# A planner change in a spectral filter + GEGLU kernel: filter-row gathers planned after the transfer transposes, and no charge for waiting on one's own engine

## The chip, the cores and the metric

The kernel runs on one core of a Trainium2 chip. The metric is the device time of one execution in microseconds (us), median of the fast executions.

## The reference, cut to what matters

```python
def reference(A_x, A_w_r, A_w_i, B_x, B_w_gate, B_w_up, B_w_down):
    x  = A_x                                   # (1, 2048, 512) bf16
    xn = _layernorm(x, axis=-1)                # no scale, no shift
    W  = w_r + 1j * w_i                        # (2048, 257) filter
    a  = irfft2(rfft2(xn) * W)                 # over both axes
    g, u = xn @ w_gate, xn @ w_up              # 512 -> 1792
    b  = (gelu(g, approximate=True) * u) @ w_down
    return x + a + b
```

## The kernel before: the parts that matter

The 2048 rows are 16 "columns" of 128 rows. VectorE makes the statistics of a column (`st`), aggregates them (`mv`), adds epsilon to the variance (`ve`); GpSimd takes the power -1/2 (`rstd`); VectorE normalises (`xn`). The columns 0 to 3 are transposed by TensorE, the others by DMA transfers. Then there are two branches: gate, up and down products, and the two-dimensional Fourier filter, built of matmuls (`bp`, `dp`, `ep`, then backwards `gp`, `yp`).

The kernel's operations are not written in the order in which they run. A planner in the source, a list scheduler with a model duration for every operation, simulates the engines and emits the operations in the order that its simulation gives:

```python
class _Plan:
    HOP = 0.1
    ...                                                     # cut
    def run(self):
        ...                                                 # cut
                for o in ops:
                    if any(d.end is None for d in o.deps):
                        continue
                    at = max([d.end + d.lag + self.HOP for d in o.deps if d.eng != "PE" or o.eng != "PE"] + [0.0])
                    ...                                     # cut: buffers, lanes; then the best priority wins
    ...
    order = plan.run()
    with tc.manual_schedule():
        for o in order:
            o.fn()
```

`at` is the planner's time at which an operation may start. It fixes only the place of the operation in its engine's queue. On the chip each engine works through its queue in order and waits for the data that an instruction really needs.

The three kinds of operation that the argument needs, with their model durations, are the normalisation chain, the fold and the gathers. The fold is four VectorE operations of 128x1024 that prepare four columns for the transform (`A`, `A`, `xf`, `xf`), followed by four groups of four `bp` matmuls that read `xf`:

```python
    def layernorm(c0, n, due, after=(), halves=1):
        for c in range(c0, c0 + n):
            s = dve(0.6, lambda c=c: stats(c), [XD[c]] + list(after), due - 3.0 + 0.01 * (c - c0))
            ag.append(dve(0.15, ..., (s,), due - 3.2))      # aggregate
        e = dve(0.07, ..., ag, due - 5)                     # ve
        r = add("POOL", 0.55, ..., (e, o_mem[1]), due - 5, lag=0.1)   # rstd: the power
        ...                                                 # then one normalisation per column, deps (r,)

    def fold(cg, t):
        ...
        a0 = dve(0.61, f0, deps, t, new=(ab,))
        a1 = dve(0.61, f1, deps + [a0], t, use=(ab,))
        a2 = dve(0.61, f2, (a0, a1), t, new=(xb,), use=(ab,))
        a3 = dve(0.61, f3, (a2,), t, use=(ab, xb))
        for q in range(4):
            ...
            p = pe(0.222, mm, (a2, a3, d_rf), t + 1, new=(sb,), use=(xb,))     # bp
            PS_[cg, q] = act(0.53, ev, (p,), t - 5, use=(sb,))                 # Bs

    for k in range(2):
        for c, s, a, n in ((2, 1, 0, 7 * KC), (0, 0, 0, KC), (1, 1, 7 * KC, KC)):
            d_tw.append(dma(P * n * 2, lambda k=k, c=c, s=s, a=a, n=n: gather(k, s, c, a, n),
                            [g_idx] + XN[11], 20, eng="POOL", issue=1.2))
```

## Time and profile before

| | before |
|---|---|
| device time | 179.18 us, three runs from 179.08 to 179.73 |
| span of the profile | 177.6 us |
| TensorE busy | 173.4 us, 1100 matmuls |
| VectorE, ScalarE, GpSimd busy | 118.1, 87.4, 18.6 us |
| idle time of TensorE | 1.34 before its first matmul, 2.68 in the tail, 0.17 in between |

### The profile page before, as it was taken

What the parts mean: (1) busy time and instruction counts of PE and PEld (TensorE: products, weight loads), DVE (VectorE), ACT (ScalarE), POOL (GpSimd) and SP (SyncE); (2) the same over time, 40 slices, a digit from 0 to 9 for tenths busy, and PEclk for the clock granted to TensorE, in tenths of its full rate; (3) what the DMA queues carried; (4) which work ended last, traced back from release to release, by engine and by line L of the source; (5) the groups of instructions that cost most, each with busy time, mean ns of one, the idle gap of its engine ahead of it and who ended that gap; (6) DMA issues with size and microseconds to landing.
All of it is one profiled execution on the core that took longest, in us unless ns stands there. A gap on an engine that the chain in (4) does not pass through costs nothing.

```text
span 177.6 us, 3041 instructions
## 1 busy us (share of the span) xinstructions
PE 173.4 (98%) x1100; PEld 92.9 (52%) x1100; DVE 118.1 (66%) x266; ACT 87.4 (49%) x158; POOL 18.6 (10%) x33
## 2 busy tenths in 40 slices
PE   6999999999999999999999999999999999999993
PEld 2598545545554544554555455554445444544463
DVE  1869999999537995889999885336442541632522
ACT  3162437456789737999998855453111211211100
POOL 3212138743200000000000000000000000000000
PEclk9999999999999999999999999999999999999999
DMA  5999487999297001302211121100222221322212
GB/s 144 311 355 359 86 270 84 223 296 193 52 347 255 2 0 29 93 2 59 61 48 37 37 59 37 27 0 0 84 68 66 83 89 59 92 80 69 74 45 59
DMA packets 23182, 19.24 MB, mean 108 GB/s; under 512 B 8512, under 2 KB 21824, under 8 KB 23168
## 3 DMA queue, kind: packets, MB, share of 16 engines
q1 hardware_dynamic: 22176, 17.57, 35.0%
q0 software_dynamic: 320, 1.19, 3.1%
q10 hardware_dynamic: 672, 0.30, 0.6%
q8 instruction: 8, 0.13, 0.3%
q14 instruction: 6, 0.05, 0.1%
HBM read 13.28 MB, written 2.10 MB: 87 GB/s over the span
## 4 chain that ended last, share of the span: by engine, by line
PE 91%; ACT 3%; DVE 3%; issue 1%; POOL 0%; DVEq 0%; POOLq 0%
PE u_ps L502 25%; PE g_ps L502 25%; PE warm L380 3%; ACT E L652 2%; PE yp L818 2%; PE bp L581 2%; PE gp L767 2%; PE yp__2078 L872 2%; PE yp__1994 L872 2%; PE yp__1967 L872 2%; PE yp__1936 L872 2%; PE yp__1909 L872 2%; PE yp__1820 L872 2%; PE yp__1793 L872 2%; PE yp__1762 L872 2%; PE yp__1735 L872 2%
## 5 line engine op out<-in xcount | busy, mean ns | idle before, releaser
L502 PE MATMUL g_ps<-xnT,Wg_sb 128*128 128x512 bf16 (+2 forms) x264 | 58.1, 347 | 0.0
L502 PE MATMUL u_ps<-xnT,Wu_sb 128*128 128x512 bf16 (+2 forms) x264 | 57.9, 347 | 0.0
L527 DVE TENSOR_TENSOR hT<-u_ps,ge 128x512 bf16<-128x512 f32 x56 | 38.4, 685 | 17.5 <-PE u_ps L502 14.4
L519 ACT ACTIVATE ge<-g_ps 128x512 bf16<-128x512 f32 x56 | 33.5, 598 | 30.5 <-PE g_ps L502 26.5
L502 PEld LDWEIGHTS <-Wu_sb 128*128 128x128 bf16 x264 | 24.3, 98 | 22.3 <-DMA Wu_sb<-in_B_w_up_dram 0.2
L502 PEld LDWEIGHTS <-Wg_sb 128*128 128x128 bf16 x264 | 24.3, 98 | 20.7 <-issue 0.2
L872 PEld LDWEIGHTS <-hT 128*128 128x128 bf16 x252 | 23.0, 98 | 21.9
L824 ACT CAST yf<-yp 128x512 bf16<-128x512 f32 x16 | 9.3, 586 | 37.6 <-PE yp L818 37.6
L652 ACT CAST E<-ep 64x512 bf16<-64x512 f32 x32 | 18.5, 579 | 1.1 <-PE ep L646 0.7
L396 DVE BATCH_NORM_STATS2 st<-x_t 128x6 f32<-128x512 bf16 x16 | 10.5, 676 | 4.8 <-DMA x_t<-in_A_x_dram 4.8
L629 ACT CAST ds<-dp 128x512 bf16<-128x512 f32 x16 | 8.8, 589 | 1.1 <-PE dp L624 1.0
L773 ACT CAST Gs<-gp 128x512 bf16<-128x512 f32 x16 | 8.6, 593 | 1.0 <-PE gp L767 1.0
L406 POOL TENSOR_TENSOR rstd<-ve,half 128x2 f32<-128x2 f32 (+2 forms) x7 | 6.6, 949 | 21.9 <-DVE ve L404 21.9
L585 ACT CAST Bs<-bp 128x512 bf16<-128x512 f32 x16 | 8.3, 603 | 0.5 <-PE bp L581 0.5
L818 PEld LDWEIGHTS <-Gs 128*128 128x128 bf16 x64 | 4.8, 98 | 3.5
L380 PE MATMUL warm<-warm 128*128 128x512 bf16 (+1 forms) x14 | 5.1, 539 | 1.3 <-POOL half L373 1.3
L412 DVE TENSOR_SCALAR xn<-x_t,mv,rstd 128x512 bf16<-128x512 bf16 (+1 forms) x17 | 6.1, 399 | 0.3 <-POOL rstd L406 0.3
L818 PE MATMUL yp<-CT,Gs 128*128 128x128 bf16 x64 | 6.0, 219 | 0.0
L683 DVE TENSOR_TENSOR m<-X,TW 128x1024 bf16<-128x1024 bf16 x8 | 5.5, 692 | 0.2
L624 PEld LDWEIGHTS <-Bs 128*128 128x128 bf16 x64 | 4.4, 98 | 2.4
L689 DVE TENSOR_TENSOR m<-X,TW 128x1024 bf16<-128x1024 bf16 x8 | 5.5, 684 | 0.0
L646 PE MATMUL ep<-ds,CT 128*128 128x512 bf16 x16 | 5.4, 379 | 0.0
(103 smaller groups left out, 169.0 us busy)
## 6 DMA issues: line engine op xcount, KB each, us to landing
y<-in_A_x_dram SPq DMA_DIRECT2D x16, 128.0 KB, 2.1
F<-F SPq DMA_DIRECT2D x32, 64.0 KB, 2.0
out_dram<-y SPq DMA_DIRECT2D x15, 128.0 KB, 1.7
Wd_sb<-in_B_w_down_dram SPq DMA_DIRECT2D x2, 896.0 KB, 8.3
x_t<-in_A_x_dram SPq DMA_DIRECT2D x3, 512.0 KB, 6.8
Wg_sb<-in_B_w_gate_dram SPq DMA_DIRECT2D x2, 512.0 KB, 6.8
Wu_sb<-in_B_w_up_dram SPq DMA_DIRECT2D x2, 512.0 KB, 9.1
Wg_sb<-in_B_w_gate_dram SPq DMA_DIRECT2D x3, 256.0 KB, 5.1
```

What stands on the lines that cost most here:

```text
L380: nc.tensor.matmul(tiles["warm"][:, 0:w], lhsT=warm[:, 0:P], rhs=warm[:, 0:w], start=True, stop=True)
L396: V.bn_stats(out=st[:], in_=x_t[:, c])
L502: nc.tensor.matmul(tiles[f"{nm}.{key}"][:, f * w:f * w + w], lhsT=W[:, e, (f0 + f) * P:(f0 + f + 1) * P], rhs=rhs(e), start=(f + e == 0), ...
L519: nc.scalar.activation(out=e[:, 0:nf * w], in_=tiles[f"g_ps.{key}"][:, 0:nf * w], func=AF.Gelu_apprx_tanh)
L527: V.tensor_tensor(out=out, in0=tiles[f"u_ps.{key}"][:, 0:nf * w].rearrange("p (f w) -> p f w", w=w) if nf > 1 else tiles[f"u_ps.{key}"][:, ...
L585: nc.scalar.copy(out=o, in_=tiles[f"bp.{cg}.{q}"][:].rearrange("p c (r g a) -> p (c r) g a", r=2, a=4))
L629: nc.scalar.copy(out=ds[:].rearrange("p (s k t) -> p s k t", s=2, t=2), in_=tiles[f"dp.{G}"][:].rearrange("p s t k -> p s k t"))
L652: nc.scalar.copy(out=tiles[f"E.{g}"][64 * h:64 * h + 64, r], in_=tiles[f"ep.{g}.{h}"][64 * r:64 * r + 64])
L773: nc.scalar.copy(out=o, in_=tiles[f"gp.{g}.{h}"][:].rearrange("p q (n a) -> p (q n) a", a=4))
L818: nc.tensor.matmul(yp[:, q], lhsT=tiles["G"][:, q, c], rhs=IQ[q], start=(q == 0), stop=(q == 3), skip_group_check=True)
L824: nc.scalar.copy(out=tiles[f"yf.{c // 2}"][:, c % 2], in_=tiles[f"yp.{c}"][:])
L872: nc.tensor.matmul(y[:, s], lhsT=tiles[sb, f][:, cl * P:(cl + 1) * P], rhs=Wd_sb[:, f, s], start=(f == 0), stop=False)
```

## The change

The intent was to keep GpSimd and the transfer rings free for the transposes that the gate and up products wait for (gathers after the last transposes, part A), and to correct a planner that charged a hand-over of 0.18 us (lag 0.08, hop 0.1) even where producer and consumer are neighbours in one engine's queue (part B). No load changes.

```diff
@@ in _Plan.run
-                    at = max([d.end + d.lag + self.HOP for d in o.deps if d.eng != "PE" or o.eng != "PE"] + [0.0])
+                    at = max([d.end + (0.0 if d.eng == o.eng and not d.nbytes else d.lag + self.HOP)
+                              for d in o.deps if d.eng != "PE" or o.eng != "PE"] + [0.0])
@@ gathers
             d_tw.append(dma(P * n * 2, lambda k=k, c=c, s=s, a=a, n=n: gather(k, s, c, a, n),
-                            [g_idx] + XN[11], 20, eng="POOL", issue=1.2))
+                            [g_idx] + [o for t in range(12, NC) for o in XT[t]], 20, eng="POOL", issue=1.2))
```

## The prediction

> **What bounds the kernel now.** I read the page's busy shares first, then busy time by stretch, then the chain of work that ended last, and only then the time-ordered instructions of GpSimd and VectorE, where the change acts.
>
> ```profile
> PE 173.4 (98%) x1100; PEld 92.9 (52%) x1100; DVE 118.1 (66%) x266; ACT 87.4 (49%) x158; POOL 18.6 (10%) x33
> ```
>
> TensorE is busy 173.4 of 177.6 us; nothing else is above 66%. The stretches (length, then busy time per engine) say where the missing 4.2 us lie:
>
> ```profile
> 0.00:1.34 1.34, 0.00 (x0) 0.00 (x1) 0.00 (x0) 0.00 (x0) 0.80 (x8) 1.00 0.00 0
> 5.78:11.50 5.72, 5.67 (x85) 5.10 (x85) 3.79 (x12) 2.06 (x4) 1.27 (x2) 1.00 1.08 327
> ...
> 27.10:36.00 8.90, 8.90 (x67) 5.00 (x65) 8.79 (x20) 5.51 (x11) 6.82 (x7) 1.00 0.85 163
> 36.00:45.00 9.00, 9.00 (x56) 4.58 (x54) 8.96 (x19) 5.46 (x11) 4.23 (x13) 1.00 1.03 228
> ...
> 69.00:85.00 16.00, 15.88 (x98) 8.17 (x97) 12.68 (x31) 15.67 (x29) 0.00 (x0) 1.00 0.23 54
> ...
> 172.00:177.60 5.60, 2.92 (x42) 2.63 (x39) 1.34 (x4) 0.00 (x0) 0.00 (x0) 1.00 0.16 47
> ```
>
> TensorE stands idle 1.34 us before its first matmul, 0.05 us in the start, 0.12 us at 69 to 85, and 2.68 us in the tail, where the last tile is added and stored. That is 4.19, all of it. VectorE is full from 27 to 45 (8.79 of 8.90, 8.96 of 9.00) without costing TensorE anything; ScalarE is full at 69 to 85 and costs 0.12. Four gate or up matmuls of 128x512 take 0.86 us in the chain, 0.216 each, at a granted clock of 1.00: this is the matmul rate and not padding. The chain leaves TensorE in one place in mid-kernel (start, length, piece):
>
> ```profile
> 63.31 0.74 PE u_ps L502 x4
> 64.05 0.34 DVE Y L693
> ...
> 75.36 0.59 ACT ds L629
> 75.99 0.38 PE gp L767 x4
> ```
>
> So the order of VectorE and ScalarE work around the first filter groups is what sits closest to the limit.
>
> **What the Trainium skill says.** (1) "Perfetto Trace Analysis", section "Identifying the Most-Contended Engine", warns that matmul busy share is a poor measure of nearness to the roofline. Here the constant 0.216 us per 512 columns shows the work is real, so I keep the reading. (2) "DMA: Bandwidth & Descriptors", section "Anatomy of one DMA", fits a transfer issued from GpSimd as 2.0 us plus bytes / 436e3. For a large gather (128 x 1799 x 2 bytes = 460 KB) that estimates 3.1 us; the trace has 3.7 to 6.2 us from issue to landing, median 4.7, and I use the trace. (3) "VectorE: DVE Perf Modes", section "The DRAIN you can't avoid", has semaphores between VectorE operations add nothing. The trace differs slightly: two independent 128x1024 additions start 0.60 us apart (42.16, 42.76), the next, which needs their result, 0.72 us later (43.48). (4) "SBUF — State Buffer", section "Who interferes with whom", has GpSimd and VectorE locking each other out of a shared port. A power over 128x4 took 1.98 us at 25.19 and 1.04 at 37.99, which fits, though VectorE was no slower during the gathers.
>
> **The change, part by part.** The kernel is a list of operations that a small planner in the source orders before emission. The planner's dependences place an operation in its engine's queue; the chip waits only for the data. So nothing is added to or removed from the chip's work: the same 1100 matmuls, the same transfers, in another order. There are two edits.
>
> *Part A, the gathers.* Six gathers of filter rows are planned after the last four transfer transposes instead of after the normalised columns 8 to 11. GpSimd now (start, length):
>
> ```profile
> 27.36 1.23 POOL L364 DMA_INDIRECT TW<-in_A_w_r_dram,idx_t  x1 [0.19 <-issue]
> ...
> 34.68 0.95 POOL L364 DMA_INDIRECT TW<-in_A_w_i_dram,idx_t  x1 [0.30 <-issue]
> 37.99 1.04 POOL L406 TENSOR_TENSOR rstd<-ve,half 128x4 f32<-128x4 f32 x1 [2.36 <-DVE ve L404]
> ...
> 43.32 0.92 POOL L611 TENSOR_TENSOR tt<-TW 128x8 f32<-128x8 bf16 x2 [1.44 <-DMA TW<-in_A_w_i_dram]
> 44.21 1.28 POOL L613 TENSOR_SCALAR TW<-tt 128x8 bf16<-128x8 f32 x4
> ```
>
> Today they take 34.68 + 0.95 - 27.36 = 8.27 us, then the last power and the table fix follow. With the new order the power comes first. A gather touches no transposed data, so on the chip it needs no landing of a transpose: it starts when the power ends, at 37.99 + 1.04 = 39.0. Issue ends at 47.3; the last starts at 46.35 and lands at 51.0 to 52.6 (4.7 to 6.2). The last two subtractions and four scalings take 45.49 - 43.32 = 2.2 us, so the fixed table is ready at 53.2 to 54.8 instead of 45.5. Its first reader:
>
> ```profile
> 55.63 0.69 DVE L683 TENSOR_TENSOR m<-X,TW 128x1024 bf16<-128x1024 bf16 x1
> ```
>
> Slack 0.8 to 2.4 us. The planner is also more pessimistic than the chip: it charges 1.2 us per gather after the transposes have landed and queues their bytes behind the down weights, so I estimate it places this multiplication at 58 to 63 of its own time. The table is therefore there first, and the price is that group 0's filter may end up to some 3 us later. Is that covered? The last inverse product (gp) of the last group runs at 114.54, the first final product (yp) that needs it at 116.72, and gate/up work lasts to 119.5; then the down projection of a column has 14 matmuls (3.02 us) that need no filter result, and the four gate/up PSUM buffers let four columns start, 12 us. A slip of 3 us is well inside. Cost on the path: 0.
>
> *Part B, no hop on the same engine.* In the planner an operation no longer waits lag plus hop (0.08 + 0.1 = 0.18 us) for one on its own engine. On the chip this wait did not exist, so nothing is saved as such; chains are just put back to back where another operation used to be slipped in. Each true dependence that becomes adjacent costs up to 0.12 us of VectorE. With 16 statistics, 16 aggregates and four folds in the full stretch, perhaps 20 new ones give at most 2.4 us, 2% of VectorE's 118. Against it: the seven row-0 operations of group 0 close up, so its filter, begun later, ends not much later than today's 68.8. The gate/up multiplications keep the highest priority and, with two PSUM buffers each, may be late: the one at 37.85 ends at 38.54, while the second-next write of such a buffer starts near 40.2, so 1.6 us late is free.
>
> At the very start order does matter:
>
> ```profile
> 5.24 0.18 DVE L403 BATCH_NORM_AGGREGATE mv<-st 128x2 f32<-128x6 f32 x1
> 5.38 0.60 DVE L412 TENSOR_SCALAR xn<-x_t,mv,rstd 128x256 bf16<-128x256 bf16 x2
> 5.90 0.15 DVE L404 TENSOR_SCALAR ve<-mv 128x1 f32<-128x1 f32 x1
> ```
>
> Working through the planner's rule by hand, the tiny variance addition (5.90) becomes ready directly after the aggregate and goes ahead of the normalisation. An addition after its aggregate starts 0.22 us later (4.23 to 4.45) and the next operation 0.07 after that, so the normalisation starts at 5.24 + 0.29 = 5.53 instead of 5.38: 0.15 us later, and TensorE waited for it (the first transposes began at 5.78, as the warm-up ended). The second column's chain is earlier by some 0.4 us, which can fill part of it. On the path: 0 to +0.15 us.
>
> Sum: 179.18 + 0 (gathers) + 0.05 to 0.15 (start) + 0 to 0.2 (new small gaps at 69 to 85) - at most 0.17 (the two gaps of today) = 179.0 to 179.5; I take 179.3.
>
> **Rivals.** *The table becomes the wait.* If the down weights' 1.8 MB, issued at 47.7, delay the last gather by 3 us or more, the table comes at 57 or 58; a VectorE queue held at that multiplication holds the gate/up multiplications, TensorE runs dry 1.6 us later, and 1 to 4 us are lost: 180 to 183. For it: DMA share 0.72 at 45 to 55. Against: the planner puts the reader later too. About 4%. *ScalarE becomes the bound.* It is 98% busy at 69 to 85; if filter groups 0 and 1 release their buffers together, copies and Gelus bunch, with gaps of 0.3 to 1 us: 179.5 to 180.2. About 15%. *The gathers were in the way and leave it.* They overlap the transposes of columns 8 to 11 and a full VectorE; moved out, VectorE could get ahead. TensorE does not wait there, so it brings at most 0.2 us: 179.0. About 30%.
>
> **Range and chances.** A gain of 2% is 3.6 us, of which reorder-able idle time offers 0.17; only the fixed start or tail could give more, and no edit touches them: 0.01. A loss of 2% takes the first rival at nearly full size: 0.03. The rest is 0.96. The three runs before spread over 0.65 us, hence a range from 178.8 to 180.4, longer upwards since all waiting can only be added.
>
> **What would show it.** Right: TensorE busy stays at 173.4 within 0.5; gathers start at about 39 directly behind the last power; the table fix ends at 53 to 55; the first table multiplication waits for VectorE's own work and not for GpSimd; the last gp lies at 114 to 118; the variance addition precedes the first normalisation. Wrong: a wait of VectorE on the table fix with TensorE idle beside it, TensorE gaps above 0.5 us at 55 to 90, gathers starting only after 43 (a wait that I think absent), or a shift of the first gate matmul (6.89) by more than 0.3 us.

## The result, and the profile after

| | before | after |
|---|---|---|
| device time, median of 6 runs | 179.39 (179.08 to 180.01) | 180.18 (179.95 to 180.51) |
| ratio after / before | | 1.0041, 95% interval 1.002 to 1.0063 |
| span of the profile | 177.6 | 178.7 |

Ratios in this document are the mean time of one kernel's fast runs over that of the other's of the same rounds, so not quite the ratio of the medians quoted. Executions over 1.5% slower than the fastest of the same kernel are left out of the means. The change is within 2%, but it is a small loss: 0.0041 x 179.4 = 0.74 us. The predicted sum, 179.0 to 179.5, has no room for it. When the two were run again in another job (e6 below) the ratio was 1.0019, with an interval from 0.9983 to 1.0054, so by times alone the loss is clear of noise in this first job only.

The busy shares of the changed kernel come first:

```profile
PE 171.9 (96%) x1082; PEld 92.4 (52%) x1100; DVE 119.4 (67%) x266; ACT 87.4 (49%) x158; POOL 16.8 (9%) x33
```

The trace has 1082 of the 1100 matmul records but all 1100 weight loads. So 171.9 is too low by 18 missing records and must not be read as less work or more idleness. Idle time has to be found as gaps between starts instead. The stretches of the changed kernel (bounds, length, then busy time of TensorE, weight loads, VectorE, ScalarE, GpSimd, clock, DMA share, GB/s) answer to those that the prediction quotes of the kernel before:

```profile
5.78:11.50 5.72, 5.05 (x80) 4.50 (x80) 4.39 (x14) 1.99 (x4) 1.29 (x2) 1.00 1.11 326
...
27.10:36.00 8.90, 8.85 (x66) 5.01 (x66) 8.83 (x19) 6.55 (x13) 0.00 (x0) 1.00 0.77 133
36.00:45.00 9.00, 8.52 (x51) 4.14 (x51) 8.60 (x18) 4.44 (x9) 6.49 (x6) 1.00 0.90 202
...
69.00:85.00 16.00, 15.78 (x87) 7.82 (x88) 15.59 (x39) 12.38 (x23) 0.00 (x0) 1.00 0.19 45
```

GpSimd is empty from 27.1 to 36 and works from 36 to 45: the gathers have moved. TensorE was busy 9.00 of 9.00 from 36 to 45 before and is 8.52 now, and VectorE, still full, has 0.40 idle. The place is visible in TensorE's time-ordered list (start, length of the group, engine, line, operation, in square brackets a wait and what ended it). Before:

```profile
41.03 1.03 PE L502 MATMUL g_ps<-xnT,Wg_sb 128*128 128x512 bf16 x4
41.89 1.06 PE L581 MATMUL bp<-RF_t,xf 128*128 128x128 bf16 x16
42.78 1.03 PE L502 MATMUL u_ps<-xnT,Wu_sb 128*128 128x512 bf16 x4
```

After:

```profile
41.38 1.03 PE L503 MATMUL g_ps<-xnT,Wg_sb 128*128 128x512 bf16 x4
42.63 0.40 PE L582 MATMUL bp<-RF_t,xf 128*128 128x128 bf16 x4 [0.22 <-DVE xf L564]
43.23 0.84 PE L582 MATMUL bp<-RF_t,xf 128*128 128x128 bf16 x12 [0.21 <-DVE xf L568]
43.91 1.03 PE L503 MATMUL u_ps<-xnT,Wu_sb 128*128 128x512 bf16 x4
```

A group's length includes the pipeline's end, so the next group starts earlier than start plus length: four gate matmuls take 0.86 us from start to next start (41.03 to 41.89), sixteen `bp` 0.89, hence four some 0.22. After the change the `bp` place in the queue comes at 41.38 + 0.86 = 42.24 and its first four start at 42.63: 0.39 us idle. The other twelve could follow at 42.63 + 0.22 = 42.85 and start at 43.23: 0.38 us. Together **0.77 us**, and both times the release is a fold operation of VectorE. (The brackets say 0.22 and 0.21, because they count from the modelled end of the matmul before.) These are the `bp` products of the columns 8 to 11. VectorE's list shows why. Before, the last two fold operations:

```profile
38.45 0.68 DVE L563 TENSOR_TENSOR xf<-A 128x1024 bf16<-128x1024 bf16 x1
...
40.32 0.72 DVE L412 TENSOR_SCALAR xn<-x_t,mv,rstd 128x512 bf16<-128x512 bf16 x2
40.96 0.68 DVE L567 TENSOR_TENSOR xf<-A 128x1024 bf16<-128x1024 bf16 x1
```

After, from the last statistics on:

```profile
35.92 0.68 DVE L397 BATCH_NORM_STATS2 st<-x_t 128x6 f32<-128x512 bf16 x1
36.64 0.18 DVE L404 BATCH_NORM_AGGREGATE mv<-st 128x2 f32<-128x6 f32 x1
36.86 0.17 DVE L405 TENSOR_SCALAR ve<-mv 128x4 f32<-128x4 f32 x1
36.94 0.69 DVE L556 TENSOR_TENSOR A<-xn 128x1024 bf16<-128x1024 bf16 x1
37.54 0.68 DVE L528 TENSOR_TENSOR hT<-u_ps,ge 128x512 bf16<-128x512 f32 x1
38.52 1.33 DVE L413 TENSOR_SCALAR xn<-x_t,mv,rstd 128x512 bf16<-128x512 bf16 x3 [0.30 <-POOL rstd L407]
...
41.90 0.67 DVE L564 TENSOR_TENSOR xf<-A 128x1024 bf16<-128x1024 bf16 x1
42.50 0.68 DVE L568 TENSOR_TENSOR xf<-A 128x1024 bf16<-128x1024 bf16 x1
```

The fold used to end at 41.64, before TensorE reached its place at 41.89. It now ends at 43.18, while TensorE reaches the place at 42.24. GpSimd's list shows the moved gathers (first and last issue) and the end of the table fix:

```profile
37.11 1.38 POOL L407 TENSOR_TENSOR rstd<-ve,half 128x4 f32<-128x4 f32 x1 [11.38 <-DVE ve L405]
38.67 1.10 POOL L365 DMA_INDIRECT TW<-in_A_w_r_dram,idx_t  x1 [0.18 <-issue]
...
46.10 1.02 POOL L365 DMA_INDIRECT TW<-in_A_w_i_dram,idx_t  x1 [0.30 <-issue]
...
49.27 0.87 POOL L614 TENSOR_SCALAR TW<-tt 128x8 bf16<-128x8 f32 x4
```

The two profiles differ by 1.1 us of span. The first down product starts at 121.10 after and at 119.98 before, so the whole 1.12 is lost before it. It is the 0.77 above and 0.35 that is net of the start, where the first column of x landed at 3.94 after and at 3.51 before. That landing is chance: the same transfer comes first in the same queue in both kernels, and the other profiles have it anywhere from 3.10 to 3.93. A second pair of profiles doesn't repeat the 0.35: the up product two places ahead of these `bp` starts at 40.16 before and 40.52 after, but at 40.13 and 40.18 in e5 and e6, the same two kernels run again. So 0.77 us is the change's own, close to the 0.74 of the timed runs.

### The profile page after: what moved, and what is told of

Same layout as the page of the kernel before. It is cut to its first block, busy times and chain, and to the rows that moved or that the text cites. A ratio compares the mean times of both kernels' runs of the same rounds, so it can differ in the third digit from the quotient of the medians.

```text
span 178.7 us, 3020 instructions
## 1 busy us (share of the span) xinstructions
PE 171.9 (96%) x1082; PEld 92.4 (52%) x1100; DVE 119.4 (67%) x266; ACT 87.4 (49%) x158; POOL 16.8 (9%) x33
## 4 chain that ended last, share of the span: by engine, by line
PE 66%; DVE 24%; issue 4%; POOL 2%; DMA 2%; ACT 1%; DVEq 0%
PE u_ps L503 15%; PE g_ps L503 14%; DVE hT L528 6%; DVE st L397 5%; DVE xn L413 2%; PE yp L819 2%; PE gp L768 2%; POOL rstd L407 2%; DMA x_t<-in_A_x_dram 2%; PE yp__2025 L873 2%; PE yp__1936 L873 2%; PE yp__1878 L873 2%; PE yp__1851 L873 2%; PE yp__1735 L873 2%; PE yp__1706 L873 2%
## 5 line engine op out<-in xcount | busy, mean ns | idle before, releaser
L503 PE MATMUL g_ps<-xnT,Wg_sb 128*128 128x512 bf16 (+2 forms) x254 | 56.7, 345 | 0.5
L407 POOL TENSOR_TENSOR rstd<-ve,half 128x2 f32<-128x2 f32 (+2 forms) x7 | 6.0, 860 | 30.4 <-DVE ve L405 30.4
L768 PEld LDWEIGHTS <-F 128*128 128x128 bf16 x64 | 4.4, 98 | 2.4 <-issue 0.2
L381 PE MATMUL warm<-warm 128*128 128x512 bf16 (+1 forms) x14 | 4.2, 457 | 1.3 <-POOL half L374 1.3
```

Source lines behind the costliest of these rows:

```text
L407: r = add("POOL", 0.55, lambda: nc.gpsimd.tensor_tensor(out=rstd[:, k], in0=ve[:, k], in1=half[:, k], op=ALU.pow), (e, o_mem[1]), due - 5, ...
L503: nc.tensor.matmul(tiles[f"{nm}.{key}"][:, f * w:f * w + w], lhsT=W[:, e, (f0 + f) * P:(f0 + f + 1) * P], rhs=rhs(e), start=(f + e == 0), ...
```

## The experiments

The main theory, called theory 1 in the expectations: part B makes the planner believe that VectorE's chains are free of cost, so that it puts the `bp` products of columns 8 to 11 too early into TensorE's queue, which then stands still. The rivals: the reordered start (the normalisation of column 0 behind the variance of column 1) costs the time; the gathers now lie beside VectorE work and slow it (part A); or the difference is disturbance, of which the kernel before has its share too. The runs were made in three jobs, each with its own runs of the kernel before; only within a job are times compared.

### e1 and e2: one part alone

e1 has part A alone, e2 part B alone.

```diff
 e1 (against the changed kernel)
-                    at = max([d.end + (0.0 if d.eng == o.eng and not d.nbytes else d.lag + self.HOP)
-                              for d in o.deps if d.eng != "PE" or o.eng != "PE"] + [0.0])
+                    at = max([d.end + d.lag + self.HOP for d in o.deps if d.eng != "PE" or o.eng != "PE"] + [0.0])
 e2 (against the changed kernel)
-                            [g_idx] + [o for t in range(12, NC) for o in XT[t]], 20, eng="POOL", issue=1.2))
+                            [g_idx] + XN[11], 20, eng="POOL", issue=1.2))
```

> The gathers are planned after the last transfer transposes, the planner's old charge for a same-engine dependence is kept. Theory 1 (the new charge put the bp products of columns 8 to 11 where VectorE's fold isn't done): no gap of TensorE at those bp products, time within 0.2 us of the kernel before (ratio 0.999 to 1.001). Theory 2 (the later gathers cost the time, by holding VectorE or by the late table): the gap of 0.6 to 0.8 us is there, ratio about 1.004. Theory 3 (start order): ratio 1.000, as the start is that of the kernel before.

> The planner's new charge alone, the gathers where they were; TensorE's, VectorE's and ScalarE's orders are those of the changed kernel until behind the fold. Theory 1: the gap at the bp products of columns 8 to 11 is there, 0.4 to 0.8 us, ratio 1.002 to 1.004; it shrinks by up to 0.3 us if part of it came from a gather beside the normalisation of columns 12 to 15 (a normalisation of 0.62 us against 0.34 to 0.41 otherwise). Theory 2: no gap, ratio 1.000.

Measured: e1 180.10 us (179.98 to 180.40), ratio 1.0004 (0.9971 to 1.0038); e2 179.98 (179.76 to 180.43), ratio 0.9997 (0.9962 to 1.0031). The kernel before ran from 179.19 to 181.29 in this job, so the ratios say little; the traces say more. e1 has no wait at the `bp` of columns 8 to 11. In e2, TensorE's list:

```profile
41.38 1.03 PE L503 MATMUL g_ps<-xnT,Wg_sb 128*128 128x512 bf16 x4
42.40 0.40 PE L582 MATMUL bp<-RF_t,xf 128*128 128x128 bf16 x4
43.00 0.84 PE L582 MATMUL bp<-RF_t,xf 128*128 128x128 bf16 x12 [0.20 <-DVE xf L568]
```

By the same reckoning the gap is (42.40 - 42.24) + (43.00 - 42.62) = 0.54 us. Part B alone makes the wait; part A alone doesn't. (The trace of e2 lacks the wait of 0.28 us at the first `gp` that the traces of before and after both have, so before its down products it loses only some 0.24 us more than the kernel before. The forecast ratio of 1.002 to 1.004 wasn't met.) What part A adds to it, 0.77 - 0.54 = 0.23, is seen in VectorE's list of e2, where the three normalisations ahead of the fold take 1.06 us instead of 1.33:

```profile
38.56 1.06 DVE L413 TENSOR_SCALAR xn<-x_t,mv,rstd 128x512 bf16<-128x512 bf16 x3 [0.34 <-POOL rstd L407]
...
42.26 0.68 DVE L568 TENSOR_TENSOR xf<-A 128x1024 bf16<-128x1024 bf16 x1
```

In the changed kernel one of the three took 0.62 us instead of some 0.4, and the first gather's issue (38.67, 1.10 long) lies on top of it. In e2 the issues of the six gathers are over by then (the last at 34.92 + 0.94 = 35.86), while their data lands until shortly before 42.67; so it is the issue, and not the transfer, that goes with the slower normalisation.

e1 has a wait that neither theory had foreseen. TensorE stands still for 0.7 us at the first `dp` (at 50.8), behind this (ScalarE's list of e1):

```profile
46.70 0.60 ACT L519 ACTIVATE ge<-g_ps 128x512 bf16<-128x512 f32 x1 [1.82 <-PE g_ps L502]
```

The gate matmuls that it waits for started at 43.90 and, at 1.03 us, ended at 44.93; the Gelu started 1.77 us after that. In the kernel before, the same Gelu started at 44.71. e5, e7, e9 and e10 come back to this.

### e3: the late products later

The theory says that only the place in the queue is wrong. So e3 makes the planner hold the `bp` of columns 8 to 11 back by 1.2 us, and edits nothing else. (What is planned behind them may move with them.)

```diff
-                              for d in o.deps if d.eng != "PE" or o.eng != "PE"] + [0.0])
+                              for d in o.deps if d.eng != "PE" or o.eng != "PE"] + [0.0]) + o.hold
             p = pe(0.222, mm, (a2, a3, d_rf), t + 1, new=(sb,), use=(xb,))
+            p.hold = 1.2 if cg == 2 else 0.0
```

> The changed kernel with the bp products of columns 8 to 11 planned 1.2 us later; the gate products go ahead of them, all else nearly as it was. Theory 1: the gap of 0.77 us is gone and nothing takes its place, time 0.6 to 0.8 us under the changed kernel, ratio to the kernel before 1.000 (0.999 to 1.001). Rival (VectorE is late in earnest and TensorE will wait for it one step on): the gap moves to another product or to the gate and up products, ratio stays near 1.004.

Measured: 180.15 us (179.93 to 180.78), ratio 1.001 (0.9975 to 1.0045), which tells the theory and its rival apart no better than the ratios of e1 and e2 did. The wait at columns 8 to 11 is gone, and half of it turns up at the next four columns, which the planner also has too early:

```profile
44.95 1.03 PE L503 MATMUL u_ps<-xnT,Wu_sb 128*128 128x512 bf16 x4
46.19 0.40 PE L582 MATMUL bp<-RF_t,xf 128*128 128x128 bf16 x4 [0.21 <-DVE xf L564]
```

The place comes at 44.95 + 0.86 = 45.81, so 0.38 us are lost here. The wait had moved; e8 repairs both places.

### e4: the start put back

e4 moves the two halves of column 0's normalisation ahead of column 1's variance addition again, and nothing else. It tests the term of the prediction for the start, +0.05 to +0.15 us.

```diff
     order = plan.run()
+    first_ve = next(o for o in order if o.eng == "DVE" and XN[1][0].deps[0].deps[0] is o)
+    for o in XN[0]:
+        order.remove(o)
+        order.insert(order.index(first_ve), o)
```

> The changed kernel with the variance addition of column 1 moved back behind the two normalisation halves of column 0; no other instruction moves on any engine. If my step on the start was right, the first transposes come 0.1 to 0.15 us sooner after the landing of x and the time falls by 0.1 us (ratio to before 1.003 to 1.004). If the earlier second column makes up for it, no change (ratio 1.004).

Measured: 180.38 us (180.05 to 180.65), ratio 1.0021 (0.9986 to 1.0055). In the changed kernel the start looks so (x lands at 3.94, variance at 5.89, then the normalisation):

```profile
5.89 0.15 DVE L405 TENSOR_SCALAR ve<-mv 128x1 f32<-128x1 f32 x1
5.96 0.59 DVE L413 TENSOR_SCALAR xn<-x_t,mv,rstd 128x256 bf16<-128x256 bf16 x2
```

The normalisation starts 2.02 us after the landing, against 5.38 - 3.51 = 1.87 before: 0.15 later, as predicted. In e4, where x landed at 3.30, it is 5.17 - 3.30 = 1.87 again. But TensorE then meets the transposes of column 1, which stand ahead of the first gate product, too early:

```profile
6.98 0.40 PE L429 MATMUL tp<-CT,xn 128*128 128x128 bf16 x4 [0.57 <-DVE xn L413]
```

The first gate product of e4 starts at 7.21, 3.91 us after the landing; in the changed kernel 7.45 - 3.94 = 3.51, in the kernel before 6.89 - 3.51 = 3.38. In the changed kernel the 0.13 are repaid, because the four transposes of column 1, 0.22 us of TensorE, are already done by then. So the start isn't the cause of the loss, and putting it back alone makes the first gate product later. Nothing of that can be seen further on: the first down product comes 117.34 us after the landing in e4, 117.16 in the changed kernel and 117.47 in its second profile (e6). The wait at `bp` was there in e4 too (0.66 us).

### e5, e6, e7: the same three kernels again

e1's late Gelu and the spread of the kernel before asked for repetition: e5 is the kernel before, once, e6 the changed one, e7 is e1's kernel.

```diff
 (no edit: before.py, after.py and e1's kernel under new labels)
```

> The kernel before once more, for a second profile. If the gap at the bp products belongs to the changed order, it is absent here again, with the bp products of columns 8 to 11 in one piece of 16; the landing of x (3.51 us in the first profile) and of the first up weights varies by some tenths from execution to execution, and TensorE's wait in the first 10 us with it.

> The changed kernel once more. If its gap is of its order, 0.6 to 0.8 us at the bp products of columns 8 to 11 again, with three normalisations beside the first gather in 1.33 us; ratio to before 1.002 to 1.005 if the later landing of x in its first profile was chance.

> The gathers alone once more. Its first profile had a Gelu 1.75 us late at 46.7 and a gap of 0.7 us at the first dp products behind it, with all engines' orders those of the kernel before up to there. If that was a chance of one execution, it is gone and the time is that of the kernel before; if the later gathers or their transfers hold up what stands there, it comes again at the same place.

Measured: e5 180.24 (one run, state unknown); e6 180.47 (180.20 to 180.60), ratio 1.0019 (0.9983 to 1.0054); e7 180.24 (179.96 to 181.54), ratio 1.0021 (0.9976 to 1.0066). The fast executions of the kernel before ran from 179.59 to 182.09 in this job, and a slow one took 182.68, which the ratios leave out; the median of all eleven is 180.01.

e6 repeats the result's trace: first `bp` 0.36 late, the other twelve 0.38, 0.74 in sum, the three normalisations 1.33 again. e7 repeats e1's: the same Gelu starts 2.3 us late at 47.01, and 0.7 us are lost at `dp`; another 0.48 are lost at the `bp` of columns 12 to 15, whose last twelve start at 46.99 instead of 46.29 + 0.22 = 46.51, behind a fold that was held up too. And e5, the kernel before, this time lost 0.87 us at the same `bp` place, with its order unchanged. Its ScalarE and TensorE lists show where that began:

```profile
36.99 1.56 ACT L585 CAST Bs<-bp 128x512 bf16<-128x512 f32 x3 [1.67 <-PE u_ps L502]
```

```profile
34.05 1.06 PE L581 MATMUL bp<-RF_t,xf 128*128 128x128 bf16 x16
...
42.93 0.84 PE L581 MATMUL bp<-RF_t,xf 128*128 128x128 bf16 x12 [0.69 <-DVE xf L567]
```

The `bp` products of 34.05 were done at 35.11, their copies to SBUF began at 36.99, and VectorE's order behind them came some 1.2 us late to the fold. So the `bp` place can be missed for two reasons: always, by the changed order, and sometimes, because ScalarE and VectorE go on late after products of TensorE that, by the profile, are long done.

### e8 and e12: both groups of products later

e8 is the changed kernel with the hold for columns 8 to 15; e12 is the same kernel in the third job.

```diff
+            p.hold = 1.2 if cg >= 2 else 0.0
```

> The changed kernel with the bp products of columns 8 to 11 and of 12 to 15 both planned 1.2 us later (the third experiment had moved half of the gap to the second of them). Theory 1 (TensorE's place for these products is all that costs): no gap above 0.1 us at bp, 0.7 us less than the changed kernel, ratio to before 0.999 to 1.001. Rival (VectorE is late for good): a gap at dp or ep instead.

> The kernel of the eighth experiment once more, in other rounds: 179.2 to 179.7 us and a ratio to before of 0.996 to 0.999 if its lead holds; no gap above 0.1 us at bp. If its lead was chance of those rounds, ratio 1.000 or more.

Measured: e8 179.34 us (179.16 to 179.70), ratio 0.996 (0.9924 to 0.9996); e12 179.57 (179.39 to 180.02), ratio 1.0006 (0.9984 to 1.0027). TensorE's list of e8:

```profile
42.67 1.03 PE L503 MATMUL g_ps<-xnT,Wg_sb 128*128 128x512 bf16 x4
43.53 1.06 PE L582 MATMUL bp<-RF_t,xf 128*128 128x128 bf16 x16
44.42 1.03 PE L503 MATMUL u_ps<-xnT,Wu_sb 128*128 128x512 bf16 x4
```

All sixteen `bp` start in one row, 0.86 us after the gate products. VectorE is no faster for it: the last fold operation of e8 starts at 42.07 and ends at 42.75, that of the changed kernel in the same job (e6) starts at 42.12 and ends at 42.80. Up to here only the place in TensorE's queue differs; behind it the hold moves other operations too, of all three engines. In the same job e8 is 180.47 - 179.34 = 1.13 us faster than the changed kernel (e6), and no run of one reaches the range of the other. That is more than the gap of 0.74. In the two profiles the first down products lie 120.91 - 119.90 = 1.01 us apart: besides the gap, e6 is 0.18 later out of the start (an up product at 38.45 against 38.27) and waits 0.18 at its first `dp`, where e8 doesn't, and e8 waits 0.08 at 40. The rest is within the rounding of these gaps. e8's lead over the kernel before did not repeat in e12: it came from executions of the kernel before that took up to 182.09 us in that job. So the change with this repair is level with the kernel before, and no version was proven better than that.

### e9 and e10: no gathers

e9 and e10 take the gathers away from the changed kernel and from the kernel before: plain loads of the same sizes take their place. They read wrong rows, so the result is wrong (relative error 0.030), but the orders of VectorE, ScalarE and TensorE are as they were.

```diff
-        nc.gpsimd.indirect_dma_start(
-            out=TW[:, k, s, a:a + n], out_offset=None, in_=w_in[:, :],
-            in_offset=bass.IndirectOffsetOnAxis(ap=idx_t[:, c:c + 1], axis=0))
+        w_rows = w_in.rearrange("(r g) k -> r (g k)", g=8)
+        nc.sync.dma_start(out=TW[:, k, s, a:a + n], in_=w_rows[128 * (c % 2):128 * (c % 2) + 128, 0:n])
```

> The changed kernel with its six gathers replaced by plain loads of the same sizes from fixed rows on the SP queue, so the result is wrong on purpose; VectorE, ScalarE and TensorE keep their instruction orders exactly. If a gather held the normalisations (1.33 us for three beside the first gather, 1.06 without), they take 1.06 and the bp gap shrinks from 0.77 to 0.5 to 0.55 us; the rest of the gap stays, as it comes from VectorE's order. If TensorE's late completion signals (up to 1.7 us, bunched, seen only while gathers ran) come from the gathers, none is seen here. Time 0.2 to 0.4 us under the changed kernel.

> The kernel before with the same replacement, wrong on purpose, orders of VectorE, ScalarE and TensorE as they were. If the gathers cause the late completion signals that gave the kernel before a bp gap of 0.9 us in its second profile, none is seen here: no gap at bp, and the six runs spread less and lie at 179.1 to 179.6. If the signals are late for another cause, the spread of 1 to 3 us stays.

Measured: e9 179.99 us (179.78 to 180.20), ratio 1.0028 (1.0007 to 1.0049); e10 179.68 (179.16 to 179.86), ratio 0.9999 (0.9978 to 1.0021). e9, VectorE and then TensorE:

```profile
37.99 1.06 DVE L412 TENSOR_SCALAR xn<-x_t,mv,rstd 128x512 bf16<-128x512 bf16 x3 [0.30 <-POOL rstd L406]
```

```profile
40.83 1.03 PE L502 MATMUL g_ps<-xnT,Wg_sb 128*128 128x512 bf16 x4
41.83 0.40 PE L581 MATMUL bp<-RF_t,xf 128*128 128x128 bf16 x4
42.43 0.84 PE L581 MATMUL bp<-RF_t,xf 128*128 128x128 bf16 x12 [0.20 <-DVE xf L567]
```

Without gathers the three normalisations take 1.06 again, and the gap is (41.83 - 41.69) + (42.43 - 42.05) = 0.52, as in e2. So the gathers, and not something else of part A, made the 0.27 us of VectorE and the 0.25 of TensorE. But a gather beside normalisations doesn't always cost this. In the kernel before, the first gather (27.36, 1.23 long) begins 0.15 us after three of them, as in the changed kernel (38.67 and 38.52), and they aren't slower:

```profile
27.21 1.06 DVE L412 TENSOR_SCALAR xn<-x_t,mv,rstd 128x512 bf16<-128x512 bf16 x3 [0.30 <-POOL rstd L406]
```

e5 and e2 repeat this, while e3, e4, e6, e8, e11 and e12 repeat the 1.33. The issue of the gather took 1.23 us in the first three and 1.10 in the others. Why the same pair costs VectorE in one place and not in the other, no run shows. e10 has no gap at this place. The two ratios differ by 0.0029, 0.52 us, which is the gap (each ratio is uncertain by 0.0021, so this is agreement and not a proof). Neither kernel had a late start behind TensorE in its trace, and e10's six runs spread over 0.70 us where the eleven of the kernel before spread over 1.20 in the same job.

### e11: a charge of 0.1 us instead of 0

If the free dependence is the fault, a charge near what the chip takes (0.12 us) should give a fold that is in time.

```diff
-                    at = max([d.end + (0.0 if d.eng == o.eng and not d.nbytes else d.lag + self.HOP)
+                    at = max([d.end + (0.1 if d.eng == o.eng and not d.nbytes else d.lag + self.HOP)
```

> The changed kernel with 0.1 us, about what the traces show, charged for a dependence on the same engine, in place of 0 (the change) and 0.18 (before). The whole order shifts, so this is no single-cause test. Theory 1: the planner places the bp products where VectorE's folds are done, gap at bp below 0.3 us, ratio to before 0.998 to 1.002. Rival: another wait takes its place and the ratio is 1.003 or more.

Measured: 180.41 us (179.90 to 180.73), ratio 1.0044 (1.002 to 1.0069). The gap at `bp` is gone, as theory 1 has it: the sixteen start at 42.09, 0.87 after the products ahead of them. But the new order has another wait, much earlier:

```profile
13.75 1.04 PE L503 MATMUL g_ps<-xnT,Wg_sb 128*128 128x256 bf16 x8
15.22 1.03 PE L503 MATMUL u_ps<-xnT,Wu_sb 128*128 128x256 bf16 x8 [0.43 <-DVE hT L528]
```

Eight such products take 0.87 (12.88 to 13.75), so 15.22 - 14.62 = 0.60 us are lost to a gate/up multiplication that VectorE has late. The right charge for one kind of dependence doesn't make the plan right elsewhere.

## Why the prediction was right, and where its sum was wrong

The range held: 180.18 is within 2% and within 178.8 to 180.4. The sum of 179.0 to 179.5 missed 0.7 us. That the range held is in part luck: its upward margin was set by the spread of the runs and for waiting in general, and the wait that came is one that the sum had put at 0. Step by step:

- **Part A, where the gathers go.** Right. They start at 38.67, behind the power, without waiting for a transpose (predicted 39.0); the last issue starts at 46.10 (predicted 46.35).
- **Part A, the table.** The fixed table is ready at 49.27 + 0.87 = 50.1, not at 53.2 to 54.8: the prediction took 4.7 to 6.2 us from issue to landing for the last gather, which are the times of the two large ones (the last is a small one and took 5.4 in the kernel before), and its data was there within 2.8 (46.10 to 48.91, where GpSimd goes on). Its first reader runs at 66.00, not 58 to 63. The table never was waited for, so the slack was 16 us, and the first rival didn't occur.
- **Part A, the slip of the filter.** "Up to some 3 us" was too little, since the first multiplication came 66.00 - 55.63 = 10.4 us later; but the last `gp` started at 116.53, inside the predicted 114 to 118, and the first down product carries only the 1.12 us that were lost earlier. The step's conclusion, that a later filter is covered, held.
- **Part A, "Cost on the path: 0".** Wrong by 0.23 us. The prediction cited the shared port ("SBUF — State Buffer", "Who interferes with whom") and set it aside because VectorE had been no slower during the gathers of before. That reading is right (1.06 us beside the first gather), but it didn't carry over to the new place, where the three normalisations take 1.33. The page names `tensor_scalar`, which the normalisation is, among the operations that can take the port pair which GpSimd needs. e9 agrees with it, the kernel before doesn't show it; that the port is the mechanism, no run shows.
- **Part B, the start.** Right in the trace: the variance goes first and the normalisation is 0.15 us later after the landing. The first gate product moved by 0.56 us, more than the 0.3 that the prediction had named as a sign of error, but 0.43 of it is the landing of x. The term itself is mostly repaid by transposes done earlier (e4). What is left, if anything, is under the scatter: at 40 us the kernel before and the changed one stand 36.65 and 36.58 us after the landing in their first profiles, 36.48 and 36.74 in their second.
- **Part B, the chains: the step that failed.** The prediction saw the mechanism: "Each true dependence that becomes adjacent costs up to 0.12 us of VectorE", at most 2.4 us. It then asked only whether the gate/up multiplications could bear that, found 1.6 us of slack in their PSUM buffers, and set the cost at 0. It didn't ask which other TensorE instructions have a place in the queue that was worked out from VectorE's planned times. The `bp` products wait for a fold directly and have no buffer in between. This term is 0.54 us in e2 and 0.52 in e9, not 0; with the late place taken away (e8) the wait is gone.
- **Part B, new gaps at 69 to 85.** Nothing lost: the gap of some 0.3 us at the first `gp` is there before (75.99) and after. Counted between starts it is 0.28 us; the 0.12 that the prediction read from busy shares is too low. ScalarE is relieved there, 12.38 us busy instead of 15.67, so the second rival fell. The third, the gathers leaving the way, brought nothing either.

How far the plan and the chip part can be read by laying the planner's own times (of its model, printed while the kernel was built) beside the trace:

| VectorE and TensorE | before: plan, chip | after: plan, chip |
|---|---|---|
| variance of columns 12 to 15 starts | 37.84, 37.74 | 35.34, 36.86 |
| first of their normalisations starts | 39.14, 39.07 | 36.63, 38.52 |
| last fold operation of columns 8 to 11 ends | 41.68, 41.64 | 41.01, 43.18 |
| their `bp` come up in TensorE's queue | 41.88, 41.89 | 41.42, 42.24 |

Before, plan and chip agree here to 0.1 us. After, TensorE is 0.82 us behind its plan and VectorE 2.17. Between the variance and the fold's end, the slip grows by 0.37 at the power (1.38 us on GpSimd where the model has 0.55; VectorE stands idle 0.30 for it) and by 0.27 at the normalisations. The chain of statistics, aggregate and variance takes 0.72 and 0.22 us from start to start where the plan now has 0.60 and 0.15. The old charge of 0.18 us per dependence was too high for the chip, but with it the plan's times were right on the whole; that the one error made up for the others is argued from this table, not tested.

The sum with the two measured terms is 179.39 + 0.54 + 0.23 = 180.16, beside the measured 180.18; that it fits so closely says little, as the medians of the kernel before differ by 0.6 us from job to job.

**What stays open.** In some executions ScalarE goes on 1.8 to 2.3 us after the end of the TensorE products that it reads (1.77 in e1, 1.88 in e5, 2.28 in e7), and gaps of 0.5 to 0.9 us follow where a queue has no slack. Whether their completion reaches it late, or another wait stands behind that the profile doesn't name, isn't known. It was seen only in kernels with gathers (a shorter one, of 1.03 us and without a gap, in e8 too), and not in the two without (e9, e10); but the first profiles of before and after, which have gathers, don't show it either. Whether the gathers cause it isn't settled. It may be part of why the fast executions of the kernel before spread from 179.0 to 182.1 us over the jobs, but no trace shows one of those above 180.3. With such a spread, ratios under 1% were read together with the trace here.

## What to carry to other kernels

Work of an engine that isn't the bottleneck is free only as long as no place in the bottleneck's in-order queue was chosen on the strength of its finishing time: for every operation that may get later, list the bottleneck's instructions that read it directly, not only those behind double buffers. Before a constant of a planner is made "truer", compare its whole chain with the trace, since one wrong charge can be making up for others (a power modelled at 0.55 us that takes 1.38). And when two totals differ by less than their spread, account for the gaps place by place.

## What the Trainium skill lacked or had wrong

- "VectorE: DVE Perf Modes", section "The DRAIN you can't avoid", measures on eight copies in a row that a semaphore after each costs nothing extra, and lacks what an operation costs that needs the result of the one before. Here that costs some 0.12 us: statistics to aggregate take 0.72 us from start to start (35.92 to 36.64), where the same statistics followed by an independent operation take 0.60 (33.37 to 33.97 in the kernel before), and aggregate to variance 0.22 instead of 0.08 to 0.10.
- "DMA: Bandwidth & Descriptors", section "Anatomy of one DMA": its fit for transfers issued from GpSimd estimates 3.1 us for a large gather; the two of the kernel before needed 6.2 and 4.7, with other transfers beside them. Beyond that, each issue held GpSimd for 0.94 to 2.32 us (e2's six).
- No page that I read has the duration of a power on GpSimd: 128x4 took 1.01 to 1.98 us.
- No page that I read tells why ScalarE can go on 1.77 us after the end of the TensorE products that it reads, in some executions only (e1).
